# Earlier loads of a batch, block-diagonal Newton steps and a moved transpose in a fused attention and SiLU kernel

## The chip, the core and the metric

The kernel runs on one core of a Trainium2 chip. The metric is the device time of one execution in microseconds; the median of several executions is compared. The engines of the core are TensorE (matmuls), VectorE, ScalarE, GpSimd and SyncE, each with an instruction stream of its own that it works off in order. They wait for one another through semaphores. In the profile they are called PE (and PEld for its weight loads), DVE, ACT, POOL and SP.

## What is computed

A Nyström attention over 8 batches of 8 heads, 576 tokens and 64 columns a head, with 32 landmarks (means of 18 neighbouring tokens), and behind it a two-layer network with SiLU.

```
q_lm, k_lm = means of q and k over 18 tokens          # 32 landmarks a head
A  = softmax(q   k_lm^T / 8)      # 576 x 32
Bm = softmax(q_lm k_lm^T / 8)     # 32 x 32
C  = softmax(q_lm k^T / 8)        # 32 x 576
Z  = Bm^T / (norm_1(Bm) * norm_inf(Bm) + 1e-6)
6 times:  Z = 2 Z - Z Bm Z        # Newton steps towards the inverse of Bm
x  = A Z C v                      # heads side by side: 4608 x 512
out = silu(x w_in) w_out          # 512 -> 2048 -> 512
```

## The kernel before

The batches are worked off one after another, two at a time in flight. For the batch whose network runs, TensorE does in each of 16 slots `s` a part of the first layer (`l1`, into `hps`, then SiLU on ScalarE into `gT`) and some matmuls of the second (`l2_mm`, into `ops`, copied by ScalarE to `ost` and stored by SP). How many of the second layer go into a slot is written out in a table (`CNT`, `REST`). Between these, the next batch's attention is done in pieces. In the code `a0` is the batch of the network, `a` the next one, `b` the number of the network's batch and `d` the slot at which the next batch's scores begin (2 for b = 0, 3 for b = 1, 0 later). The whole order is written out by hand: each engine executes its instructions in the order in which the program issues them, so the place of a line in the code is the place in each engine's queue.

The pieces of one batch that the change and the prediction's steps touch:

- Loads (`load_qk` L101, `load_v` L112, `load_w_in` and `load_w_out` L142 to L150). They are issued on GpSimd, q and k of one batch as four transfers in the order k, q (heads 0 to 3), k, q (heads 4 to 7) into `nat`, and convert float32 to bf16 on the way. `nat` and `v` have two buffers each. At the start of the kernel both weights, batch 0 and 1's q, k and v and then batch 2's stand in one row in this queue. Each issue waits, on GpSimd, for the transfer eight issues before it in this queue.
- Landmarks of batch 2 and later (`landmarks_pool`, L223 to L238): five additions on GpSimd (`lma`, `lmb`, `lmc`, `lmd`, `lmn`) for heads 0 to 3, then five for heads 4 to 7. VectorE then transposes the result (`lm_t`, `lmc` L271), and the scores of batch 2 (`a_pair`, `sa`, L621; called at L991 in slot 3 of b = 1) need it.
- `transpose_qk` (L199): VectorE transposes one of the four loaded pieces, 1.2 us each.
- Bm and the Newton steps: `b_norm` (L321), `f_mm` (L336), `b_scale` (L350), `f_out` (L374), `ns_mm` (L382), `ns_step` (L401), `x_out` (L413), `w_scale` (L481), `w_mm`, `w_out` (L508), `z_mm` (L521), `z_out` (L537). Eight heads are two groups of four. With `self.tiled` the four heads of a group are four separate 32 x 32 matmuls on four quadrants of the array, eight small matmuls in a step; the state `fx` is 128 x 128. Without it the four matrices stand on the diagonal of one 128 x 128 operand (`bdt`, then `fx` with 128 x 320), two large matmuls in a step. Before the change batches 0 and 1 are tiled and batches 2 to 7 are not.
- The products of A (`a_norm`, with `a_mul` on GpSimd, L696): they divide the exponentials by their row sums (`arec`, VectorE). `a0.a_norm(1)` and `(2)` (L1050, L1051, slot 4 of b = 0) finish A of batch 0, which TensorE transposes in `a0.a_transpose(1)` (slot 6).
- `m_pair` (L757): the product of w_in with a batch's Z C v, whose PSUM results VectorE and ScalarE copy to `mb` ("the w_in copies"). It shares a PSUM bank (tag "a") with `a_transpose`.

In slot 4 of b = 0 the program issues, on GpSimd, `load_v(2)` (L1049), then the two products of batch 0's A, and at the end of the slot `load_qk(2)` (L1182). The four transfers of `load_qk(3)` follow in slots 5 to 9 (L1062 to L1104), then the landmarks of batch 2 (L1105, L1112).

Of the kernel before, what the change touches and what calls it, by code (L numbers as in the profile page):

```python
# [43 lines left out]
def kernel(  # L44
# [41 lines left out]
    def psa1(nm, dt=FP):  # L86
        return psa.tile([128, 512 if dt == FP else 1024], dt, tag="a", name=nm)
# [156 lines left out]
    class Att:  # L244
        def __init__(self, b):
            self.b = b
            self.qkT, self.v, self.lmn = qkT_t[b], v_t[b], lmn_t[b]
            self.bd = bd_t[b % 2]


            self.tiled = b < 2
            self.by_dma = b >= 2

            self.sub = b >= 2

            self.early = b >= 4

            self.mean = b < 2

            self.split = SPLIT[b]  # L260
            self.lmc = attp.tile([128, 4, L, 2], BF, tag="lmc", name="lmc")
            self.bb = None
            self.m_done = 0
            self.csum = attp.tile([128, 2], FP, tag="csum", name="csum")
            self.eCT, self.t = [None, None], [None, None]
            self.s, self.sa, self.w = [None, None], [None] * 3, [None, None]
            self.fx = None
# [582 lines left out]
    ORD = (1, 0, 3, 2)  # L850
# [18 lines left out]
    a = Att(0)  # L869
# [67 lines left out]
    for b in range(B):  # L937
# [4 lines left out]
        a, ready = ready, None  # L942
# [4 lines left out]
        def l1(s):  # L947
            h[s] = l1_mm(b, s)

        def act(s):  # L950
            l1_act(b, s, h.pop(s))

        for s in range(NDC):
# [3 lines left out]
            if s <= d and b == 0:  # L957
# [14 lines left out]
                if s == 0:  # L972
                    a = Att(1)
# [3 lines left out]
            elif not nxt or s <= d:  # L977
# [6 lines left out]
                if b == 1 and s == d:  # L984
                    a = Att(2)
# [9 lines left out]
            elif s == d + 1:  # L995
                l1(s)
                act(s)
                l2_mm(cnt[s])
                if b == 0:

                    transpose_qk(1, ORD[s])
                    a.lm_t(1)
                    a.bd_expand(0, 2, nc.gpsimd.tensor_copy)
                    for i in (1, 2):
                        a0.a_scores(i)
                        a0.a_max(i)
                a.b_scores()
                a.c_scores()
                a.b_max()
                a.c_max(0)  # L1010
                table(AF.Exp)
                if b == 0:
                    for i in (1, 2):
                        a0.a_shift(i)
                        a0.a_exp(i)
                a.b_exp()
            elif s == d + 2 and a.sub:
                a.a_start()
                a.c_max(1)
                a.c_exp(0)  # L1020
                a.c_exp(1)
                a.a_exp_all()
                a.b_norm()
                l2_mm(cnt[s])
                table(AF.Silu)
                l1(s)
            elif s == d + 2:
                n = cnt[s]
                a.a_start()
                a.a_scores(0)  # L1030
                a.a_scores(1)
                a.c_max(1)
                a.a_max(0)
                a.a_max(1)
                a.c_exp(0)
                a.c_exp(1)
                a.a_scores(2)
                a.a_max(2)
                for i in range(2):
                    a.a_shift(i)  # L1040
                    a.a_exp(i)
                a.b_norm()
                a.a_shift(2)
                a.a_exp(2)
                table(AF.Silu)
                a0.m_unit(2, nc.vector.tensor_copy, nc.vector.tensor_copy, pair=True)
                a.c_transpose(0)
                a.c_out(0)
                load_v(2)  # L1049
                a0.a_norm(1)  # L1050
                a0.a_norm(2)  # L1051
                a.f_mm()
                a.b_scale()
                a.f_out()
                l2_mm(n)
                l1(s)
            elif b == 0:
                l1(s)
                r = s - d
                n = cnt[s]  # L1060
                if r == 3:
                    load_qk(3, (1,))  # L1062
                    act(s - 1)
                    a0.m_unit(3, nc.scalar.copy, nc.scalar.copy, parts=2,
                              between=lambda: act(s))
                    nc.vector.tensor_tensor(out=parity, in0=mask[:, 0:2, 0],
                                            in1=mask[:, 2:4, 0], op=OP.add)
                elif r == 4:
                    a.ns_mm()
                    a.ns_step()  # L1070
                    act(s)
                    a0.a_transpose(1)
                    a0.a_out(nc.scalar.copy)
                    a.c_transpose(1)
                    a.c_out(1)
                    a.a_norm(0)
                    load_qk(3, (0,))
                elif r == 5:
                    act(s)
                    a.ns_mm()  # L1080
                    a.ns_step()
                    a.w_scale()
                    a.a_norm(1)
                elif r == 6:
                    a.ns_mm()
                    a.ns_step()
                    act(s)
                    l2_mm(2)
                    n -= 2
                    a.ns_mm()  # L1090
                    a.a_norm(2)
                    a.ns_step()
                    load_qk(3, (3,))
                elif r == 7:
                    a.ns_mm()
                    a.ns_step()
                    act(s)
                    l2_mm(2)
                    n -= 2
                    a.w_mm()  # L1100
                    a.w_out()
                    a.ns_mm(last=True)
                    a.x_out()
                    load_qk(3, (2,))  # L1104
                    landmarks_pool(2, 0)  # L1105
                elif r == 8:
                    a.z_mm(psa1("zt"))
                    a.z_out()
                    act(s)
                    l2_mm(n)  # L1110
                    n = 0
                    landmarks_pool(2, 2)  # L1112
                    a.a_transpose(0)
                    a.a_out(nc.vector.tensor_copy)
                    transpose_qk(2, ORD[0])
                elif r == 10:
                    a.a_transpose(1)
                    a.a_out(nc.vector.tensor_copy)
                    transpose_qk(2, ORD[1])
                elif r > 11:  # L1120
                    transpose_qk(2, ORD[r - 10])
                if s in h:
                    act(s)
                if r in (9, 11):
                    a.m_pair(r - 9)
                l2_mm(n)
            elif s == d + 3:
                l1(s)
                act(s - 1)
                act(s)  # L1130
                l2_mm(2)
                a.f_mm()
                a.b_scale()
                a.f_out()
                a.w_scale()


                nc.gpsimd.tensor_copy(out=gate, in_=a.wsp[:, 0, :])  # L1138
                l2_mm(cnt[s] - 2)
                a.ns_mm()  # L1140
            elif s <= d + 8:
                l1(s)
                if s == d + 6:
                    a.w_mm()
                a.ns_step()
                act(s)
                if s == d + 4:
                    a.a_sum(0)
                elif s == d + 5:
                    a.a_sum(1)  # L1150
                elif s == d + 6:
                    a.w_out()
                    a.a_rec(0, 2)
                    a.a_mul(0)
                    a.a_mul(1)
                l2_mm(cnt[s])
                a.ns_mm(last=(s == d + 8))
            elif s == d + 9:
                l1(s)
                a.x_out()  # L1160
                act(s)
                l2_mm(cnt[s])
            elif s == d + 10:
                l1(s)
                a.z_mm()
                a.z_out()
                act(s)
                l2_mm(cnt[s])
            else:
                l1(s)  # L1170
                act(s)
                if nxt and s in mp:
                    a.m_pair(2 * mp.index(s))
                n = cnt[s]
                if s == 15 and ready and ready.early:
                    l2_mm(3)
                    n -= 3
                    ready.a_pair()
                l2_mm(n)
            if b == 0:  # L1180
                if s == 4:
                    load_qk(2)  # L1182
            elif b + 2 < B:

# [56 lines left out]
```

## Time and profile before

| | us |
|---|---|
| median of 3 executions | 263.85 |
| lowest and highest | 263.08, 264.89 |
| the profiled execution | 264.01 |
| its span, first to last instruction | 262.3 |
| busy in the span: TensorE | 249.8 |
| ScalarE | 170.4 |
| VectorE | 165.0 |
| GpSimd | 133.4 |

The profiled execution's time is 1.7 us longer than its span and 0.16 us over the median. All times of single instructions below are counted from the start of the span. The views used are: the page (shares and groups), the chain of work that ended last, the timeline of one engine (start, length, line, operation, output<-inputs with forms, count, and in brackets the idle time of the engine before it and what ended that), the busy times by stretch (for each engine busy time and count; then the granted TensorE clock as a share of full speed, the share of the DMA engines and GB/s), and the DMA view, which gives the time from issue to landing.

### The profile page before, as it was taken

The page shows a single profiled execution, that of the slowest core. Times are in us where ns is not written, and L with a number is a line of the kernel's source. Part 1 is how long each engine was busy: PE and PEld are TensorE (multiplying, and loading weights), DVE is VectorE, ACT ScalarE, POOL GpSimd, SP SyncE. Part 2 cuts the span into 40 slices and gives each one's busy share as a digit, 9 for nine tenths or more (in the row PEclk, how much of TensorE's full clock was granted, in tenths as well). Part 3 has the DMA queues.
Part 4 walks back from the last instruction along what each step waited for, and adds up shares of the span by engine and source line. Part 5 has one row for each costly group of instructions (what it writes and reads, how often), then busy time and mean ns, then how long its engine had stood idle before and what let it go on. Part 6 is the DMA issues. An engine that isn't in the chain of part 4 may idle for free.

```text
span 262.3 us, 6655 instructions
## 1 busy us (share of the span) xinstructions
PE 249.8 (95%) x2765; PEld 138.0 (53%) x2765; DVE 165.0 (63%) x391; ACT 170.4 (65%) x315; POOL 133.4 (51%) x161
## 2 busy tenths in 40 slices
PE   8989899968999999999999999999999999999994
PEld 2646555433554456555645565556555665555553
DVE  5778974926797678967886779776977754000000
ACT  2278974664957595769675967597577957446511
POOL 7706276595399839962994199237933030100000
PEclk9999999997999999999999999999999999999999
DMA  7999999950439991896279726213441411121122
GB/s 217 201 210 207 206 206 213 223 133 2 100 69 226 202 182 42 130 182 141 80 104 177 127 90 86 88 30 115 83 87 42 104 40 42 40 80 42 41 80 81
DMA packets 30062, 31.16 MB, mean 119 GB/s; under 512 B 10960, under 2 KB 21456, under 8 KB 30032
## 3 DMA queue, kind: packets, MB, share of 16 engines
q0 software_dynamic: 14816, 17.76, 41.4%
q1 hardware_dynamic: 15216, 12.98, 16.6%
q8 instruction: 21, 0.34, 0.5%
q14 instruction: 9, 0.07, 0.1%
HBM read 36.70 MB, written 9.44 MB: 176 GB/s over the span
## 4 chain that ended last, share of the span: by engine, by line
PE 73%; POOL 11%; DVE 5%; DMA 5%; issue 3%; ACT 1%; POOLq 0%; ACTq 0%
PE ops L80 40%; PE hps L80 19%; DMA nat<-in_q_dram 5%; POOL lma L229 4%; PE idle L80 3%; PE bb L80 2%; PE lmp L80 2%; PE sa L80 2%; POOL lmb L232 2%; POOL lmc L234 2%; PE mp L80 1%; PE scp L80 1%; DVE cmx L448 1%; POOL nat L108 1%; PE mpp L80 1%
## 5 line engine op out<-in xcount | busy, mean ns | idle before, releaser
L80 PE MATMUL ops<-w_out_sb,gT 128*128 128x512 bf16 (+1 forms) x592 | 147.9, 376 | 0.2 <-DMA w_out_sb<-in_moe_w_out_dram 0.2
L807 ACT ACTIVATE gT<-hps 128x576 bf16<-128x576 f32 (+2 forms) x128 | 82.6, 652 | 60.3 <-PE hps L80 59.7
L80 PE MATMUL hps<-AT,mb 128*128 128x288 bf16 (+2 forms) x512 | 82.8, 286 | 0.8 <-ACT gT L807 0.6
L80 PEld LDWEIGHTS <-gT 128*128 128x128 bf16 x592 | 54.0, 98 | 49.3 <-issue 10.3
L80 PEld LDWEIGHTS <-mb 128*128 128x128 bf16 x512 | 48.6, 98 | 27.2 <-issue 1.1
L203 DVE STREAM_TRANSPOSE qkT<-nat 128x576 f32<-128x576 f32 x32 | 39.0, 1241 | 0.8 <-DMA nat<-in_k_dram 0.5
L833 ACT COPY ost<-ops 128x512 f32<-128x512 f32 (+1 forms) x37 | 21.1, 571 | 14.3 <-PE ops L80 14.0
L229 POOL TENSOR_TENSOR lma<-nat 128x1152 f32<-128x1152 bf16 x12 | 28.5, 2377 | 2.9 <-DMA nat<-in_q_dram 2.8
L407 DVE SCALAR_TENSOR_TENSOR fx<-fx,bb 128x320 bf16<-128x320 bf16 (+1 forms) x39 | 17.0, 435 | 11.4 <-PE bb L80 11.2
L773 DVE CAST mb<-mp 128x512 bf16<-128x512 f32 x28 | 18.0, 684 | 7.2 <-PE mp L80 7.2
L635 POOL TENSOR_TENSOR xs<-xs,nm 128x576 f32<-128x576 f32 x12 | 13.6, 1153 | 15.1 <-DVE nm L630 15.1
L165 ACT ACT_TABLE_LOAD x16 | 20.5, 1283 | 1.1 <-PEq L1225 0.8
L1138 POOL COPY gate<-wsp 128x2 f32<-128x2 f32 x6 | 1.1, 184 | 30.8 <-DVE wsp L492 30.8
L691 POOL TENSOR_TENSOR an<-ex,arec 128x576 bf16<-128x576 bf16 x12 | 13.6, 1158 | 5.3 <-DVE arec L677 5.3
L80 PEld LDWEIGHTS <-fx 32*32 32x32 bf16 (+1 forms) x168 | 8.2, 93 | 12.0 <-DVE fx L407 4.4
L774 ACT CAST mb<-mpp 128x1024 bf16<-128x1024 f32 x14 | 14.2, 1012 | 0.1
L80 PE MATMUL bb<-fx 32*32 32x64 bf16 (+2 forms) x168 | 13.1, 205 | 0.5 <-DVE fx L407 0.3
L626 DVE STREAM_TRANSPOSE xs<-sa 128x576 f32<-128x576 f32 x12 | 8.7, 762 | 6.6 <-PE sa L80 6.6
L448 DVE TENSOR_REDUCE cmx<-scp 128x1 f32<-128x576 f32 x16 | 12.0, 753 | 1.0 <-PE scp L80 0.7
L234 POOL TENSOR_TENSOR lmc<-lmb,lma 128x384 f32<-128x384 f32 x12 | 12.0, 999 | 0.9
L232 POOL TENSOR_TENSOR lmb<-lma 128x384 f32<-128x384 f32 x12 | 12.0, 996 | 0.9
L80 PEld LDWEIGHTS <-lmc 32*32 32x32 bf16 x576 | 6.3, 91 | 10.5 <-DVE lmc L271 5.2
(125 smaller groups left out, 267.2 us busy)
## 6 DMA issues: line engine op xcount, KB each, us to landing
out_dram<-ost SPq DMA_DIRECT2D x35, 256.0 KB, 2.0
v<-in_v_dram POOLq DMA_DIRECT2D x8, 576.0 KB, 6.9
nat<-in_k_dram POOLq DMA_DIRECT2D x15, 288.0 KB, 7.0
nat<-in_q_dram POOLq DMA_DIRECT2D x15, 288.0 KB, 8.3
w_in_sb<-in_moe_w_in_dram POOLq DMA_DIRECT2D x4, 512.0 KB, 15.1
w_out_sb<-in_moe_w_out_dram POOLq DMA_DIRECT2D x4, 512.0 KB, 13.8
raw<-in_k_dram SPq DMA_DIRECT2D x1, 576.0 KB, 3.9
raw<-in_q_dram SPq DMA_DIRECT2D x1, 576.0 KB, 5.0
```

The costliest lines, as they stand in the source:

```text
L80: nc.tensor.matmul(out=o, lhsT=lhsT, rhs=rhs, start=start, stop=stop, skip_group_check=True)
L165: nc.scalar.activation(out=spare[:, 1:2], in_=spare[:, 0:1], func=func)
L203: nc.vector.transpose(out=o.rearrange("p (l t) -> p t l", t=SEG), in_=nat_t[b][:, j, :].bitcast(FP).rearrange("p (t l) -> p t l", l=L))
L229: nc.gpsimd.tensor_tensor(out=a1, in0=nat[:, :, 0:3 * w], in1=nat[:, :, 3 * w:6 * w], op=OP.add)
L232: nc.gpsimd.tensor_tensor(out=a2, in0=a1[:, :, 0:w], in1=a1[:, :, w:2 * w], op=OP.add)
L234: nc.gpsimd.tensor_tensor(out=a3, in0=a2, in1=a1[:, :, 2 * w:3 * w], op=OP.add)
L407: nc.vector.scalar_tensor_tensor(out=n, in0=self.fx, scalar=2.0, in1=self.p, op0=OP.mult, op1=OP.add if self.tiled else OP.subtract)
L448: nc.vector.tensor_reduce(out=mx, in_=self.s[g][:, :, 0:HF], op=OP.max, axis=AX.XY, negate=True)
L773: nc.vector.tensor_copy(out=o[:, r, 0:512], in_=m[r])
L774: nc.scalar.copy(out=o[:, :, 512:1024], in_=m2)
L807: nc.scalar.activation(out=gT_t[b][:, 2 * s:2 * s + 2, o + c0:o + c1], in_=h[:, :, 0:c1 - c0], func=AF.Silu)
L833: nc.scalar.copy(out=ost[:, 0:hi - lo], in_=st["ps"][:, 0:hi - lo])
```

## The change

Three edits:

- `self.tiled` is now true for batch 0 alone, so batch 1's Newton steps, and what leads into them and out of them, use the block-diagonal operands. `z_mm` needs no bank of its own then.
- `transpose_qk(2, ORD[0])` in slot 11 of b = 0 (r = 9) is issued behind `m_pair`, so on VectorE it stands behind the two w_in copies and not ahead of them.
- `load_qk(2)` is issued at the end of slot 3 of b = 0 and not of slot 4. In GpSimd's queue the four issues now stand ahead of `load_v(2)` and of the products `a0.a_norm(1)` and `(2)`; before, they stood behind all three.

```diff
-            self.tiled = b < 2
+            self.tiled = b < 1
...
                 elif r == 8:
-                    a.z_mm(psa1("zt"))
+                    a.z_mm()
...
                     a.a_transpose(0)
                     a.a_out(nc.vector.tensor_copy)
-                    transpose_qk(2, ORD[0])
                 elif r == 10:
...
                 if r in (9, 11):
                     a.m_pair(r - 9)
+                if r == 9:
+                    transpose_qk(2, ORD[0])
                 l2_mm(n)
...
             if b == 0:
-                if s == 4:
+                if s == 3:
                     load_qk(2)
```

On the engines this changes, for batch 1:

```
TensorE  f_mm      8 matmuls 32x32          ->  2 of 128x128
         ns_mm     8 of 32x64 (5 times)     ->  2 of 128x160
         ns_mm     8 of 32x32 (the last)    ->  2 of 128x32
         z_mm      8 of 32x32               ->  2 of 128x64
VectorE  b_norm    + bdt (128x256)
         b_scale   cs, n, reciprocal, 1 multiply -> cs, n, + 1e-6, reciprocal, 2 multiplies
         f_out     128x64   -> 128x256
         ns_step   128x128  -> 128x320 (5 times)
         w_scale   + wsp (128x4)
         w_out     + wz (128x256)
         x_out     1 of 128x64 -> 2 of 64x64
         z_out     2 of 128x64 -> 1 of 128x128
ScalarE  w_out     - 2 scaled copies (128x64)
```

## Prediction

> **What bounds the kernel now.** I read the page first: TensorE is busy 95% of 262.3 us, so a gain must come from its gaps or its clock. Then the chain that ended last, which leaves TensorE for GpSimd between 36 and 60 us:
>
> ```profile
> 36.35 12.13 DMA nat<-in_q_dram
> 48.62 2.38 POOL lma L229
> ...
> 57.70 1.00 POOL lmc L234
> 60.15 0.49 PE sa L80 x16
> ```
>
> A load of batch 2's q lasts 12.13 us from issue to use, two landmark sums (L229 to L237) follow on GpSimd, then batch 2's first scores `sa`. Third, TensorE's timeline, for the price:
>
> ```profile
> 56.16 0.81 PE L80 MATMUL ops<-w_out_sb,gT 128*128 128x512 bf16 x3
> 60.15 0.70 PE L80 MATMUL sa<-qkT,lmc 32*32 32x288 bf16 x32 [3.19 <-DVE lmc L271]
> ```
>
> TensorE has nothing to do from 56.97 to 60.15, the kernel's longest gap. Fourth, the busy times in stretches of 1 us (TensorE's granted clock is the third number from the end):
>
> ```profile
> 60.00:61.00 1.00, 0.85 (x33) 0.48 (x34) 0.43 (x2) 0.00 (x0) 0.73 (x1) 1.00 0.00 0
> 62.00:63.00 1.00, 1.00 (x4) 0.23 (x2) 1.00 (x3) 0.59 (x1) 0.17 (x1) 0.50 0.00 0
> 64.00:65.00 1.00, 1.00 (x18) 0.28 (x3) 0.55 (x2) 0.99 (x6) 1.00 (x1) 0.50 0.00 0
> 66.00:67.00 1.00, 1.00 (x7) 0.47 (x5) 0.86 (x6) 0.98 (x4) 0.00 (x0) 1.00 0.00 0
> ```
>
> The gap is followed by some 3.5 us at half clock. Fifth, GpSimd's timeline, which says why the sums are late:
>
> ```profile
> 27.62 0.78 POOL L114 DMA_DIRECT2D v<-in_v_dram  x1
> 34.16 1.62 POOL L696 TENSOR_TENSOR an<-ex,arec 128x512 bf16<-128x512 bf16 x2 [5.76 <-DVE arec L681]
> 45.27 0.53 POOL L108 DMA_DIRECT2D nat<-in_q_dram  x1 [2.30 <-DMA v<-in_v_dram]
> 48.62 2.37 POOL L229 TENSOR_TENSOR lma<-nat 128x1152 f32<-128x1152 bf16 x1 [2.83 <-DMA nat<-in_q_dram]
> ```
>
> GpSimd idles before both, so transfers set its time. By issue plus time to landing (the DMA view in narrow windows), loads land one behind another in issue order: w_in[3] 29.0, w_out 31.5, 34.0, 36.7 and 39.1, v(1) 42.05, v(2) 45.02, batch 2's four at 46.85, 48.45, 49.9 and 51.3.
>
> **Part 1: the four loads ahead of v(2) and ahead of the products of A.** The queue is backed up, so issuing early brings nothing by itself; the order does. Batch 2's loads no longer follow v(2), whose transfer took 45.02 - 42.05 = 2.97 us. They land 2.97 sooner: 43.9, 45.5, 46.9, 48.3; v(2) lands near 51 and is first read at 73.5 (`wp`), which hides it. GpSimd's last issue before the sums (45.27) now waits for batch 2's k (43.9) in place of v(2), so it is free at 44.7. The sums start at 48.62 - 2.97 = 45.65, the second at 51.25 (its loads land by 48.3), and `sa` can start at 60.15 - 2.97 = 57.18. Bounds: 2.6 and 3.3 us sooner, since an output store at 41.7 shares the engines.
>
> The price is paid by what stands behind on GpSimd. An issue waits for the load eight before it in this queue (45.27 waited for v(2)). So batch 2's issues wait for nothing, w_in[2] (26.5), w_in[3] (29.0) and w_out[0] (31.5), and v(2)'s for w_out[1] (34.0, seen 0.25 later). It takes 0.8, and the products move from 34.16 to 35.05 and end at 36.67 in place of 35.78, 0.89 later. TensorE's transposes of them stood at 36.16; part 2 holds TensorE until 36.6 anyway, and only the third transpose needs the second product, so I count 0.0 more; without that cover it is 0.5. SP's queue is moved past by nothing.
>
> **Part 2: batch 1's Newton steps on block-diagonal operands.** Prices are from batch 1's and batch 2's rows in one trace:
>
> ```profile
> 36.26 0.29 DVE L407 SCALAR_TENSOR_TENSOR fx<-fx,bb 128x128 bf16<-128x128 bf16 x1 [0.46 <-PE bb L80]
> 40.97 0.24 PE L80 MATMUL bb<-fx 32*32 32x64 bf16 x8
> 66.91 0.29 DVE L316 TENSOR_TENSOR bdt<-bmt,mask 128x256 bf16<-128x256 bf16 x1
> 69.96 0.30 PE L80 MATMUL bb<-fx 128*128 128x160 bf16 x2
> 70.30 0.49 DVE L407 SCALAR_TENSOR_TENSOR fx<-fx,bb 128x320 bf16<-128x320 bf16 x1 [0.61 <-PE bb L80]
> ```
>
> VectorE gains `bdt` (0.24 from start to start), a longer scaling (cs to f_out: 1.30 against 0.82), f_out 0.42 against 0.22, five steps at 0.49 against 0.29, `wsp` 0.17, `wz` 0.36 (ScalarE sheds 0.52 at 43.56), two `xb` for one x (+0.23), and saves 0.14 in z_out: some 2.5 us. TensorE's eight small matmuls took 0.17 a step, the two large ones 0.14: six steps save 0.2, z_mm 0.13. What reaches TensorE:
> - First step: 0.24 + 0.48 + 0.20 = 0.92 later, ready at 36.4 against TensorE's 35.97: 0.46.
> - At 39.20 TensorE already waited 0.25 for w_out[3], which swallows 0.25 of it.
> - Fourth step (40.97): its operand is behind arec and the third step on VectorE. The eCT copy is 0.4 late, the second step adds 0.20, `wsp` 0.17, the third step 0.20, so the operand comes at 41.65: TensorE is 0.69 late, in place of the 0.2 before.
> - Fifth step, `wz`, `xb`: ready before TensorE asks (`xb` 45.0, z_mm 45.16), because the output matmuls and w_mm lie between. With z_mm's saving, TensorE is 0.39 late at 45.2.
> Bounds: 0.1, if the rest of the slack of 0.3 to 0.5 in these waits absorbs it, and 2.5 + 0.9 = 3.4, if every added instruction and the products stand in its way.
>
> **Part 3: batch 2's first transpose behind the w_in copies.** TensorE's timeline at 48.73:
>
> ```profile
> 48.73 0.64 PE L724 MATMUL atp<-ident,an 128*128 128x128 bf16 x4 [0.55 <-DVE mb L773]
> ```
>
> It waited 0.55 for the first `mb` copy, which stood behind the 1.26 us transpose at 46.89. With the copies first, the bank is free at 47.8, TensorE comes at 48.18 + 0.39 = 48.57: it gains 0.55 and the net of parts 2 and 3 is -0.16. The transpose moves to 48.35; what is late behind it is the copy of the next AT piece, at 49.9 in place of 49.77, needed by the next w_in product at 50.2; all four transposes end near 54.6, before the sums end (56.7). Bounds: 0 and 0.55.
>
> **The sum.** TensorE reaches batch 2's scores at 56.97 - 0.16 = 56.8; their operand is there at 57.18. So they start at 57.18, 2.97 sooner, and the gap shrinks to 0.4. At a gap of 0.65 (86.04, before batch 3's scores) the clock stayed at 1.00, so here too. The half clock cost TensorE 1.92 us: from 60.78 to 67.91 it did work that by batch 3's rows takes 0.43 + 0.49 + 0.43 + 0.72 + 2.16 + 0.98 = 5.21, in 7.13. But little of that comes out: VectorE's reductions waited 0.45 for `scp` and are then bound by `nm` before them, and ScalarE's exponentials, table load and first gT after it (hps at 70.82 waited for it 0.56) move only that 0.47. TensorE will wait some 1.7 us there. VectorE's wsp, which frees GpSimd for batch 3's sums (gate, 69.75), moves 0.67 because f_mm is no longer late, and through them the scores at 86.69. After that each batch has the same order. Gain 2.97 + 0.67 = 3.64: the profiled execution's 264.01 becomes 260.37. It stands 0.16 over the median of 263.85, so the forecast is **260.2 us**. Its own range: at best the gap closes wholly and TensorE comes at 56.97 - 0.55 + 0.1 = 56.5, which with 0.9 behind it gives 259.3; at worst 2.6 + 0.47, and TensorE late by another 0.4, gives 261.2.
>
> **Rivals.**
> - Newton on the path. If half of the 3.4 us reaches TensorE, it comes to the scores at 56.97 - 0.55 + 1.7 = 58.1 and the gain is 2.03 + 0.47 = 2.5 at most: 261.4; with all of it, 263.05. For it: VectorE is nearly full from 28 to 36. Against: from 36 to 47 it is half idle, and waits for `bb` there.
> - The clock falls again, after the new wait of 1.7 us. A drop costs up to 1.92, of which 0.4 is absorbed before batch 3's scores: 264.01 - 3.64 + 1.5, so 261.7 as a median. Rows bound it: 0.65 idle kept the clock, 3.19 halved it; 1.7 is nearer to the first. [...]
> - The loads gain nothing: if v(2)'s packets and batch 2's were served together, q lands no earlier and the time is 263.8. Against: landings a whole transfer apart, in order.
> - Slower, by the same sharing one step earlier. If batch 2's loads, now queued at 28 to 32, share with w_out, w_out[1] to [3] land up to four transfers of 1.45 = 5.8 us later. Then v(2)'s issue holds the products until about 40.8 and TensorE stands at its transposes 5.4 us, with half clock behind it (1.92): the scores start at 62 and the time is 264.01 + 1.9 + 1.9 - 0.7, so 266.9. It turns to a loss once TensorE loses over 60.15 - 56.42 + 0.67 = 4.4 us. Against: the order of landings again.
>
> **How the numbers follow.** Forecast 0.62, Newton on the path 0.15, clock 0.10, no gain 0.06, slower 0.07. About 1% (2.6 us) is what a measurement of this kernel can tell from no change. Below 261.2 lie the forecast and a third of the next two: faster 0.70; same 0.23; slower 0.07. The range 259.3 to 262.2 takes in the forecast and most of Newton and clock.
>
> **What would show it.** Right: batch 2's `lma` near 45.6, `sa` near 57.2 with an idle below 0.6, clock 1.00 from 61 to 66, hps after the Silu table waiting for gT over 1 us, no wait for `mb` at the second A transpose. Wrong: `sa` waiting for nothing but late (Newton), products of A after 36, a clock below 1.00 after 68, or `w_out_sb` waits longer than 0.3.

## The result and the profile after

| | before | after |
|---|---|---|
| median of 4 executions, us | 264.24 | 260.66 |
| lowest and highest, us | 263.08, 264.89 | 259.94, 261.40 |
| the profiled execution and its span, us | 264.01, 262.3 | 260.70, 259.0 |

The ratio is 0.9869, with a 95% interval of 0.9823 to 0.9916: 3.6 us faster. The profiles of two kernels start up to 0.2 us apart (the sum cs at L352, which follows the same reciprocal in all of them, stands at 34.41 before and at 34.21 to 34.37 in nine later profiles), so differences of 0.2 us between stamps are not read below.

The chain that ended last has lost most of its GpSimd part (11% before):

```profile
PE 77%; DVE 10%; POOL 4%; issue 3%; ACT 3%; DMA 2%; ACTq 0%
```

TensorE's timeline after. The lines are batch 1's first and fourth Newton step, batch 1's second A transpose, batch 2's scores, the first layer behind the Silu table, and batch 3's scores:

```profile
37.43 0.31 PE L80 MATMUL bb<-fx 128*128 128x160 bf16 x2 [1.58 <-DVE fx L377]
...
42.78 0.32 PE L80 MATMUL bb<-fx 128*128 128x160 bf16 x2 [0.99 <-DVE fx L407]
...
49.27 0.65 PE L724 MATMUL atp<-ident,an 128*128 128x128 bf16 x4
...
57.53 0.70 PE L80 MATMUL sa<-qkT,lmc 32*32 32x288 bf16 x32
...
67.65 0.65 PE L80 MATMUL hps<-AT,mb 128*128 128x288 bf16 x4 [0.74 <-ACT gT L807]
...
83.34 0.70 PE L80 MATMUL sa<-qkT,lmc 32*32 32x288 bf16 x32 [0.47 <-DVE lmc L271]
```

Batch 2's scores come 2.62 us sooner (60.15 before) and wait for nothing: the gap of 3.19 us is gone, and TensorE itself is now the last to arrive. The wait for `mb` (0.55) is gone too. But two waits of VectorE's `fx`, 1.58 and 0.99, are new. Batch 3's scores are 3.35 sooner (86.69 before), and the rest of the kernel follows at that distance: the span is 3.3 shorter. The clock, third number from the end, stays at 1.00 where it was at 0.50:

```profile
62.00:63.00 1.00, 1.00 (x6) 0.48 (x5) 0.93 (x4) 0.94 (x5) 0.48 (x1) 1.00 0.00 0
64.00:65.00 1.00, 0.93 (x7) 0.59 (x7) 0.86 (x6) 1.00 (x3) 0.00 (x0) 1.00 0.53 106
```

GpSimd's timeline after:

```profile
31.70 0.53 POOL L108 DMA_DIRECT2D nat<-in_q_dram  x1 [2.01 <-DMA w_out_sb<-in_moe_w_out_dram]
34.54 0.80 POOL L114 DMA_DIRECT2D v<-in_v_dram  x1 [2.31 <-DVE cs L352]
35.40 1.61 POOL L696 TENSOR_TENSOR an<-ex,arec 128x512 bf16<-128x512 bf16 x2
...
44.69 0.54 POOL L108 DMA_DIRECT2D nat<-in_q_dram  x1
45.24 2.38 POOL L229 TENSOR_TENSOR lma<-nat 128x1152 f32<-128x1152 bf16 x1
```

The issues stand still for earlier loads, as forecast: batch 2's fourth for w_out[0], and v(2)'s until 34.5. The bracket of v(2)'s names VectorE's cs, but cs is nothing that a load needs; w_out[1], the load eight before it, lands at 21.03 + 12.9 = 33.93 (DMA view), shortly before. So the products of A start 1.24 later than before. The sums start at 45.24, 3.38 sooner, and without a wait: q had landed at 28.04 + 16.7 = 44.74 (DMA view), and GpSimd was still busy.

VectorE's timeline shows what the products did. First the two scalings as batch 2 has them in the kernel before, then the kernel after:

```profile
68.05 0.37 DVE L370 TENSOR_SCALAR fx<-bm,nrm 128x32 bf16<-128x32 bf16 x2
```

```profile
34.85 0.46 DVE L367 TENSOR_SCALAR n<-n 128x2 f32<-128x2 f32 x1
...
35.54 1.51 DVE L370 TENSOR_SCALAR fx<-bm,nrm 128x32 bf16<-128x32 bf16 x2
36.96 0.41 DVE L377 TENSOR_TENSOR fx<-bb,nrm 128x256 bf16<-128x256 f32 x1
...
56.47 0.31 DVE L271 STREAM_TRANSPOSE lmc<-lmn 128x128 f32<-128x128 f32 x1 [1.01 <-POOL lmn L237]
```

The two scalings at L370 took 0.37 in batch 2, and here 1.51: they begin just behind the start of the first product (35.40) and end at 37.05, with the second (37.01). These 1.14 us more are what makes batch 1's first Newton step miss its forecast, 37.43 for 36.4. The last line: the landmarks are ready at 56.78, 0.75 before TensorE asks.

### The profile page after: what moved, and what is told of

The parts are those of the page before. It is cut to its first block, busy times and chain, and to the rows that moved or that the text cites. A ratio compares the mean times of both kernels' runs of the same rounds, so it can differ in the third digit from the quotient of the medians.

```text
span 259.0 us, 6520 instructions
## 1 busy us (share of the span) xinstructions
PE 241.9 (93%) x2676; PEld 137.7 (53%) x2717; DVE 168.3 (65%) x396; ACT 169.9 (66%) x313; POOL 133.2 (51%) x161
## 4 chain that ended last, share of the span: by engine, by line
PE 77%; DVE 10%; POOL 4%; issue 3%; ACT 3%; DMA 2%; ACTq 0%
PE ops L80 42%; PE hps L80 22%; PE bb L80 3%; PE lmp L80 2%; PE mp L80 2%; PE sa L80 2%; DMA raw<-in_k_dram 2%; DVE cmx L448 2%; PE wp L80 1%; PE scp L80 1%; PE mpp L80 1%; POOL lma L229 1%; DVE nm L609 1%; POOL nat L108 1%; DVE arec L662 1%
## 5 line engine op out<-in xcount | busy, mean ns | idle before, releaser
L80 PE MATMUL ops<-w_out_sb,gT 128*128 128x512 bf16 (+1 forms) x555 | 139.6, 373 | 4.4 <-issue 4.0
L407 DVE SCALAR_TENSOR_TENSOR fx<-fx,bb 128x320 bf16<-128x320 bf16 (+1 forms) x39 | 17.9, 459 | 11.0 <-PE bb L80 10.9
L80 PE MATMUL bb<-fx 128*128 128x160 bf16 (+2 forms) x132 | 13.5, 212 | 3.6 <-DVE fx L407 1.7
L80 PEld LDWEIGHTS <-fx 128*128 128x128 bf16 (+1 forms) x132 | 8.4, 94 | 14.1 <-DVE fx L407 5.3
L662 DVE TENSOR_REDUCE arec<-ex 128x18 f32<-128x576 bf16 (+2 forms) x17 | 11.7, 689 | 0.0
```

The costliest lines, as they stand in the source:

```text
L80: nc.tensor.matmul(out=o, lhsT=lhsT, rhs=rhs, start=start, stop=stop, skip_group_check=True)
L407: nc.vector.scalar_tensor_tensor(out=n, in0=self.fx, scalar=2.0, in1=self.p, op0=OP.mult, op1=OP.add if self.tiled else OP.subtract)
L662: nc.vector.tensor_reduce(out=r, in_=x, op=OP.add, axis=AX.X)
```

## The experiments

Theory L: the place of batch 2's loads in the queue gives the gain, and the Newton steps cost. Rival N: the Newton steps bring it, and the loads are hidden anyway. First each part alone, and the whole without Newton.

**Loads alone.**

```diff
-                if s == 4:
+                if s == 3:
                     load_qk(2)
```

> Batch 2's four loads moved alone; Newton steps and transpose as before. Theory L (the order of the loads in GpSimd's queue gives the gain): batch 2's first sum starts at 45.2 to 45.6 in place of 48.6, its scores at 57.0 to 57.3 in place of 60.15, no half clock behind them, and the kernel is 3.3 to 4.0 us faster than before. The products of A are late by 1.2 us, but no scaling of VectorE is slowed by them for over 0.3 us, since the tiled form has none of the two tensor_scalars. Rival N (the block-diagonal steps bring the gain, the loads are hidden anyway): under 1 us faster.

Measured: median 259.65, ratio 0.9835 (0.9798 to 0.9871). GpSimd's timeline, and then TensorE's:

```profile
44.62 2.36 POOL L229 TENSOR_TENSOR lma<-nat 128x1152 f32<-128x1152 bf16 x1 [0.68 <-DMA nat<-in_q_dram]
```

```profile
56.45 0.70 PE L80 MATMUL sa<-qkT,lmc 32*32 32x288 bf16 x32
```

The whole gain is here, 4.8 us by the medians where 3.3 to 4.0 was expected, though the interval overlaps that of the change; N falls. Sums and scores are 0.6 sooner than expected: q lands at 28.04 + 16.5 = 44.54 (DMA view), 3.9 us sooner than before, not 2.97 (more on that in the last two experiments).

**Newton steps alone.**

```diff
-            self.tiled = b < 2
+            self.tiled = b < 1
...
-                    a.z_mm(psa1("zt"))
+                    a.z_mm()
```

> Batch 1's block-diagonal Newton steps alone. Theory L: batch 2's scores wait for the same landmark sums as before, at 60.1, so what TensorE loses before (0.5 to 1.6 us at the first step, 2 us at the fourth) only shrinks its gap of 3.2 us to 1.5 to 2.7; the time is within 0.7 us of before, and faster by the 0.5 to 0.7 if the clock stays at 1.00 behind the shorter gap. Rival N: 1.5 us faster or more, the scores earlier than 59.5.

Measured: 264.32, ratio 1.0005 (0.9985 to 1.0026). TensorE's timeline:

```profile
36.26 0.31 PE L80 MATMUL bb<-fx 128*128 128x160 bf16 x2 [0.45 <-DVE fx L377]
...
41.60 0.31 PE L80 MATMUL bb<-fx 128*128 128x160 bf16 x2 [0.50 <-DVE fx L407]
...
60.35 0.70 PE L80 MATMUL sa<-qkT,lmc 32*32 32x288 bf16 x32 [3.22 <-DVE lmc L271]
```

The time is unchanged, but my picture was too dark: the fourth step is 0.63 late and not 2, nothing of it is left at the scores, and the gap does not shrink. With the products of A back at 34.1, the first step costs 0.3.

**Transpose alone.**

```diff
-                    transpose_qk(2, ORD[0])
...
                     a.m_pair(r - 9)
+                if r == 9:
+                    transpose_qk(2, ORD[0])
```

> Batch 2's first transpose behind the w_in copies, alone. Theory L: TensorE no longer waits 0.55 for the first mb copy, arrives 0.55 earlier at batch 2's scores, and waits there 3.7 in place of 3.2; the time is that of before within 0.3 us. Rival (TensorE is the bound throughout): 0.5 us faster.

Measured: 264.47, ratio 1.0014 (0.9995 to 1.0032). TensorE's timeline:

```profile
59.97 1.16 PE L80 MATMUL sa<-qkT,lmc 32*32 32x288 bf16 x32 [3.71 <-DVE lmc L271]
```

The 0.55 saved reappears whole as a longer gap. A stall ahead of a larger one is worth nothing.

**Loads and transpose, no Newton.** Both edits above (the first and the third).

> Loads and transpose moved, batch 1's Newton steps tiled as before: the whole change without its Newton part. Theory L with the cost of the Newton part as the trace of the changed kernel shows it (TensorE 0.7 us late at batch 2's scores): scores at 56.8 to 57.0, 0.4 to 0.7 sooner than in the changed kernel, bound by the sums, and 3.8 to 4.3 us faster than before. Rival N: slower than the changed kernel, scores later than 57.5.

Measured: 259.45, ratio 0.9835 (0.9791 to 0.9879). TensorE's timeline, and VectorE's beside GpSimd's:

```profile
56.07 0.70 PE L80 MATMUL sa<-qkT,lmc 32*32 32x288 bf16 x32
```

```profile
34.95 1.07 DVE L363 TENSOR_TENSOR fx<-bm,nrm 128x64 bf16<-128x64 bf16 x1
35.95 0.21 DVE L377 TENSOR_TENSOR fx<-bb,nrm 128x64 bf16<-128x64 f32 x1
```

```profile
34.90 1.62 POOL L696 TENSOR_TENSOR an<-ex,arec 128x512 bf16<-128x512 bf16 x2
```

The scores come 1.46 sooner than with Newton, more than twice the 0.4 to 0.7 that I expected. And even the tiled form's one scaling (0.22 before) took 1.07 when it began just after the first product, and ended as that ended (34.90 + 1.04 = 35.94). The next instruction, with an operand from PSUM, ran its 0.21 beside the second product. In the run with the loads alone the same scaling began at 34.95, ahead of the product at 35.16, and took 0.22:

```profile
34.95 0.22 DVE L363 TENSOR_TENSOR fx<-bm,nrm 128x64 bf16<-128x64 bf16 x1
```

The next four ask whether it is order or earliness that counts, what held VectorE, and what the half clock was worth.

**Order only.** Nothing is issued sooner; v(2) goes behind batch 2's loads at their old place.

```diff
-                load_v(2)
                 a0.a_norm(1)
...
                 if s == 4:
                     load_qk(2)
+                    load_v(2)
```

> The kernel before with one edit: the load of v(2) is issued behind batch 2's four loads, at their old place (slot 4, behind the products of A), so nothing is issued sooner and only v(2) changes its place in the queue. Theory O (order, not earliness): q of batch 2 lands about 3 us sooner, the first sum starts at 45.2 to 45.8, the scores at 56.9 to 57.3, and the kernel is 3.5 to 4.0 us faster than before, with the products of A at 34.2 as before. Rival E (earlier issue counts): the sums start at 48 or later and the time is within 1 us of before.

Measured: 259.45, ratio 0.9810 (0.9795 to 0.9825). GpSimd's timeline, and TensorE's:

```profile
34.00 1.62 POOL L696 TENSOR_TENSOR an<-ex,arec 128x512 bf16<-128x512 bf16 x2 [6.48 <-DVE arec L681]
35.57 0.62 POOL L108 DMA_DIRECT2D nat<-in_k_dram  x1
...
37.76 0.84 POOL L114 DMA_DIRECT2D v<-in_v_dram  x1
...
44.81 2.37 POOL L229 TENSOR_TENSOR lma<-nat 128x1152 f32<-128x1152 bf16 x1 [0.68 <-DMA nat<-in_q_dram]
```

```profile
56.36 0.70 PE L80 MATMUL sa<-qkT,lmc 32*32 32x288 bf16 x32
```

Batch 2's loads are issued 8 us later than in the changed kernel and land at the same time (q at 36.19 + 8.5 = 44.69 against 44.74, DMA view). Theory O stands: the queue is backed up here, and only the order in it counts. This one moved line has the lowest ratio of all kernels here; its interval just touches that of the change and overlaps those of the other kernels with the new order.

**Products of A ahead of v(2), in the changed kernel.**

```diff
-                load_v(2)
                 a0.a_norm(1)
                 a0.a_norm(2)
+                load_v(2)
```

> The changed kernel with v(2)'s load issued behind the two products of A, so GpSimd does not wait for w_out before them. Theory P (the products, 1.2 us later, hold VectorE's two scalings of the Newton start at 35.5, 1.51 us in place of 0.37): products at 34.2 to 35.8, the scalings done by 36.3 in place of 37.05, the first Newton step on TensorE at 36.5 to 36.9 in place of 37.43, the scores of batch 2 at 56.8 to 57.2, 0.3 to 0.7 us faster than the changed kernel. Rival Q (the scalings are slow for another reason): they take 1.5 again and the first step stays at 37.4.

Measured: 259.79, ratio to before 0.9829 (0.9804 to 0.9853). VectorE's timeline, and TensorE's:

```profile
35.41 0.49 DVE L370 TENSOR_SCALAR fx<-bm,nrm 128x32 bf16<-128x32 bf16 x2
```

```profile
36.28 0.31 PE L80 MATMUL bb<-fx 128*128 128x160 bf16 x2 [0.45 <-DVE fx L377]
...
41.62 0.31 PE L80 MATMUL bb<-fx 128*128 128x160 bf16 x2 [0.70 <-DVE fx L407]
...
56.53 0.70 PE L80 MATMUL sa<-qkT,lmc 32*32 32x288 bf16 x32
```

With the products out of the way the scalings take 0.49, and the first and fourth step stand at 36.28 and 41.62, where the prediction had 36.4 and 41.65. The scores come 1.0 sooner than in the changed kernel; step and scores are 0.2 to 0.3 sooner than expected. P stands, Q falls.

**One scaling in place of two, in the changed kernel.**

```diff
             nc.vector.reciprocal(out=self.nrm, in_=n1)
+            if self.b == 1:
+                nc.vector.tensor_tensor(
+                    out=self.fx[:, :, w:w + L], in0=self.bm,
+                    in1=self.nrm.unsqueeze(2).to_broadcast((128, 2, L)), op=OP.mult)
+                return
             for g in range(2):
...
```

> The changed kernel with batch 1's Newton start scaled by one tensor_tensor (128x64) in place of two tensor_scalars (128x32). Theory P (an instruction of VectorE is held until the running product of GpSimd ends, and each of the two was held by one product): the single one is held to the end of the first product at 36.4 and ends near 36.6, or is not held and ends near 35.8; the first Newton step stands at 36.5 to 37.1 in place of 37.43. Rival S (the engines share and both run slower all along): it takes 0.8 us or more and still ends near 37.

Measured: 260.35, ratio 0.9846 (0.9826 to 0.9866). VectorE's timeline, and GpSimd's:

```profile
35.21 0.96 DVE L370 TENSOR_TENSOR fx<-bm,nrm 128x64 bf16<-128x64 bf16 x1
36.09 0.41 DVE L382 TENSOR_TENSOR fx<-bb,nrm 128x256 bf16<-128x256 f32 x1
```

```profile
35.05 1.61 POOL L701 TENSOR_TENSOR an<-ex,arec 128x512 bf16<-128x512 bf16 x2
```

The scaling ends at 36.17; the first of the two products takes 1.04 of the 1.61 and ends at 36.09. So one instruction is held by one product, and the next (f_out, here L382) runs its usual 0.41 beside the second. The first Newton step stands at 36.56. S asked for 0.8 or more and an end near 37; the length came, the end did not, it is the product's; S falls.

**Filled gap, in the kernel before.**

```diff
                         n -= 3
+                        if b == 1:
+                            idle(psa1("fill"), 13, 512)
                         a.a_pair()
```

> The kernel before with 13 matmuls of 128x512 on a zero operand ahead of batch 2's scores, in TensorE's gap of 3.2 us; they write a bank that nobody reads. Theory C (the half clock costs little of its own, since VectorE's reductions and ScalarE's table load bound the next 10 us): scores again at 60.1, clock 1.00 behind them, hps behind the Silu table at 70.3 in place of 70.8, and 0.3 to 0.9 us faster than before. Rival H (the half clock costs its whole 1.9 us): 1.6 us faster or more.

Measured: 263.43, ratio 0.9967 (0.9945 to 0.9990). TensorE's timeline:

```profile
56.47 2.97 PE L80 MATMUL fill<-zero 128*128 128x512 bf16 x13
59.84 0.70 PE L80 MATMUL sa<-qkT,lmc 32*32 32x288 bf16 x32 [0.41 <-DVE lmc L271]
60.48 0.60 PE L80 MATMUL ops<-w_out_sb,gT 128*128 128x512 bf16 x2
...
66.87 0.59 PE L80 MATMUL ops<-w_out_sb,gT 128*128 128x512 bf16 x2
...
69.97 0.65 PE L80 MATMUL hps<-AT,mb 128*128 128x288 bf16 x4 [0.74 <-ACT gT L807]
```

The clock stays at 1.00. From the scores to hps it takes 10.13 us, as in the changed kernel (10.12), against 10.67 before. The work between the two `ops` lines takes 6.39 us (60.48 to 66.87) and not the 7.13 of before (60.78 to 67.91): 0.74 of TensorE's time comes back, where the prediction had priced 1.92. The kernel gets 0.8 us back by the medians, 0.3 to 1.5 by the interval. C stands, H falls.

**Two combinations.** The first is loads and transpose with the products ahead of v(2), the second order only with the transpose; batch 1 is tiled in both.

> The changed kernel without its Newton part and with v(2)'s load issued behind the products of A: loads of batch 2 early, transpose moved, batch 1 tiled. Theory P and L together: products of A at 34.1, no VectorE instruction held beside them for over 0.5 us, first Newton step at 35.8 to 36.0, sums at 44.4 to 44.9, scores at 55.9 to 56.3, 0.3 to 0.6 us sooner than the changed kernel with the products first (56.53), which prices block-diagonal steps without their collision; 4.6 to 5.2 us faster than before. Rival: that pair of edits does not add up, scores at 56.5 or later.

> The kernel before with v(2)'s load behind batch 2's loads at their old place, and batch 2's first transpose behind the w_in copies; nothing else. Theory O: the transpose, worth nothing alone because the scores waited for the sums, is now worth up to 0.3 us, until the sums bind again: scores at 55.9 to 56.3 against 56.36 without it, 4.8 to 5.3 us faster than before. Rival: TensorE regains nothing, scores at 56.3 to 56.5.

Measured: 259.60, ratio 0.9830 (0.9802 to 0.9858), and 259.62, ratio 0.9818 (0.9798 to 0.9838). TensorE's timeline of the one, then the other:

```profile
56.66 0.70 PE L80 MATMUL sa<-qkT,lmc 32*32 32x288 bf16 x32 [0.25 <-DVE lmc L271]
```

```profile
56.45 0.70 PE L80 MATMUL sa<-qkT,lmc 32*32 32x288 bf16 x32
```

Both are 4.8 us faster than before, as expected, but the scores come later: by 0.4 us in the first, which is where its rival had them, and by 0.15 in the second, too little to decide. The loads landed a little later here (sums at 45.12 and 44.90), and w_out was waited for 0.59 and 0.48, so the transpose buys nothing that can be measured. In the six kernels with the new order but without the collision of block-diagonal scalings and products, the scores stand at 56.07 to 56.66; whether they could come sooner is not shown.

**The first output store, in the kernel before.** Why did q land 3.9 sooner, with the loads alone, and not 2.97?

```diff
-                nc.sync.dma_start(out=..., in_=ost...)
+                late.append((r0, lo, hi, ost))
+                if (b, c0) != (0, 0):
+                    for r0, lo, hi, ost in late:
+                        nc.sync.dma_start(out=..., in_=ost...)
+                    late.clear()
```

> The kernel before with the first output store, issued at 41.7 beside the loads of batch 2, issued together with the second one at 54. The batch 2 loads then land with nothing beside them. Theory D (q landed 4.0 sooner in the changed order and not the 2.97 of v(2)'s transfer, because k and q also left the stretch that the store shares, 42 to 49): the sums start 0.6 to 1.0 sooner than before, at 47.6 to 48.0, and the scores at 59.1 to 59.5. Rival V (v(2) itself takes 4.0 there): the sums start within 0.2 us of 48.5.

The edit did not move the store: it stood first in SyncE's queue and was issued at 41.51 all the same. The run only shows how two runs of one order agree: ratio 0.9995 (0.9977 to 1.0012), sums at 48.32. The next one takes `reversed(late)`.

> As the last one, with the two stores in the other order in SyncE's queue, so that the first output store stands behind the second and is issued at about 54 in place of 41.5; in the last kernel it waited only for its own copy and was issued at 41.51 as before. Theory D: with no store beside them, batch 2's k and q land sooner, the first sum starts at 47.6 to 48.0 (before: 48.4 to 48.6, two profiles), the scores at 59.0 to 59.5. Rival V: the sums start within 0.2 us of 48.4.

Measured: the stores at 53.4, ratio 0.9940 (0.9917 to 0.9963). GpSimd's timeline, and TensorE's:

```profile
47.69 2.36 POOL L229 TENSOR_TENSOR lma<-nat 128x1152 f32<-128x1152 bf16 x1 [2.12 <-DMA nat<-in_q_dram]
```

```profile
59.21 0.70 PE L80 MATMUL sa<-qkT,lmc 32*32 32x288 bf16 x32 [2.90 <-DVE lmc L271]
```

The sums start 0.6 to 0.9 sooner (48.32 and 48.62 with the store beside the loads), so the store is most of the missing 0.9. D stands. That the executions are 1.4 us faster in the median (263.05 against 264.45), more than this profile shows, stays open; three of the seven, at 262.38 to 262.64, show a mean granted clock of 0.997 or 0.998, the other four, the profiled one among them, 0.992 or 0.993.

## Why the prediction was right

260.2 was forecast, 260.66 measured; a gain of 3.64 against 3.6. The mechanism is the one named, but two of its terms were off and cancelled: that the number came so close is luck in part.

- What bounds it: right. The scores waited for landmark sums, those for loads, those for v(2) ahead of them. Order only shows it with a single line.
- Loads: 2.97 was v(2)'s transfer alone; q landed 3.7 us sooner here (44.74 against 48.45), and 3.9 with the loads alone. The term missed the output store, which was only taken as a bound (2.6 to 3.3) and lies outside it: the sooner k and q are through before most of the store (before, it was issued at 41.69 and landed 7.3 later; here at 42.46 and 6.0 later). GpSimd's own queue gave back 0.3 (the sums start 0.50 behind q's landing, 0.17 before), so the sums started 3.38 sooner.
- Products of A: their delay was seen (0.89; it was 1.24) but costed at 0.0, because the transposes behind them were covered. This step failed. The work that paid was on another engine: VectorE's scalings (L370) ran into them, 1.51 for 0.37.
- Newton: the steps' own prices were right, 36.28 and 41.62 where the products are out of the way; but there, too, two errors cancel at the first step: `bdt` did not delay cs (it starts 0.12 behind the reciprocal ahead of it with `bdt` as without), and the products still lengthened the addition at L367 to 0.35 and the scalings to 0.49 (0.17 and 0.37 in batch 2). With the collision TensorE was 1.46 late at the first step (0.46 forecast), 1.81 at the fourth (0.69), and still 0.56 at the scores, where the forecast had it 0.16 early. So the rival "Newton on the path" came true by 0.7 us, through the products and not through VectorE's load. The gain is that of the loads: no run here shows that the Newton steps bring time.
- Transpose: the wait of 0.55 went, and alone it is worth nothing, as far as the scores waited for the sums anyway.
- The sum: scores at 57.53 for 57.18. The sums were ready 0.4 sooner than forecast, TensorE 0.7 later; the later of the two counts.
- Behind the scores: hps waited 0.74, not 1.7, since TensorE came later than worked out: the work behind the scores, 5.21 by batch 3's rows, takes 6.39 even at full clock (filled gap), 0.20 of it a wait for ScalarE's `eC`. The clock held. From the scores to batch 3's scores 0.73 was won (25.81 against 26.54), 0.67 forecast; the filled gap alone gave 0.74.
- The slower rival: TensorE never waited for w_out in the changed kernel (the longest wait for it in the other kernels is 0.59), and loads landed in order.

## What to carry to other kernels

When transfers stand in a backed-up queue, ask which of them is needed last and put that one last; issuing sooner cost the issuing engine its waits here (2.01 and 2.31 us) and brought nothing (q at 44.74, against 44.69 when issued 8 us later). When work on GpSimd moves in time, look at what VectorE does at its new place, not only at who waits for it (here 0.37 became 1.51). And price a gap by what ends it: a stall removed ahead of it comes out only as far as no other engine binds there (here 0 of 0.55), and a faster clock behind it is worth only what the stretch then takes less, its waits included (here 0.8 of the 1.92 priced).

## What the hardware showed that was not expected

- The VectorE scalings of this kernel, which read all their operands from SBUF, were held until about the end of a GpSimd product that had begun just before them: two that take 0.37 together took 1.51, held by a product each (end at 37.05, the second product's at 37.01), one of 0.22 took 1.07 (36.02, the first product's at 35.94), and the one scaling put in for the two took 0.96 (36.17 and 36.09). One that began 0.2 us ahead of the product (loads alone: 34.95 and 35.16) was not held and took 0.22, nor was f_out, which reads PSUM (0.21 at L377 and 0.41 at L382, each beside the second product). Why the ones were held and the others not is not shown.
- A gap of 2.90 us halved the granted clock as well (last experiment: 0.50 from 60.0 to 63.4), as did 3.19 (the kernel before), 3.22 (Newton steps alone), 3.29 (the store that did not move) and 3.71 (transpose alone); waits of up to 1.58 (the first Newton step after the change, 1.00 from 33 to 45) did not. The half clock itself lasted some 3.4 us each time, by the busy times in stretches of half a us (before, for one: 61.8 to 65.2).
